# Another order for the first block: input weight, gate products and next attention

## The chip, the cores and the metric

The program runs on one core of a Trainium2 chip. The metric is the device time of one execution in microseconds (us); lower is better. TensorE multiplies (PE in the rows, PEld its weight loads), VectorE (DVE) and ScalarE (ACT) work on single elements and empty PSUM, GpSimd (POOL) helps with element work on SBUF, and SyncE (SP) issues the DMAs. Each engine takes its instructions strictly in the order in which they were recorded, and waits at the first whose inputs or buffers are not ready.

## The reference

Three layers follow each other on 8 batches of 576 rows and 512 features:

```
attn:  per head (8 x 64) and chunk of 64 rows:  softmax(q k^T / 8) v
moe:   h = relu(x @ w_in)              # 512 -> 1024, first half u, second half v
       v_n = (v - mean(v)) / sqrt(var(v) + 1e-6)
       v_s = w_spatial @ v_n + b_spatial[:, None]      # over the 576 rows
       x = (u * v_s) @ w_out                           # 512 -> 512
moe2:  u = x + (relu(x^T @ w_tok1) @ w_tok2)^T         # over the 576 rows
       out = u + relu(u @ w_ch1) @ w_ch2               # 512 -> 1536 -> 512
```

The moe weights arrive as 64-bit floats: as pairs of 32-bit words that the kernel turns into 32-bit floats itself.

## The kernel before

Every matrix is held as a sum of a rounded "hi" part and the remainder "lo", and each product is three matmuls (hi hi, hi lo, lo hi). Attention and the gated layer run block by block, one batch each: while TensorE does the gated layer of batch b, the other engines do the softmax of batch b+1 piece by piece. The order is written out by hand as three strings of words: `FIRST` (lines 24 to 36: attention of batch 0, gated layer of batch 0, conversion of the weights, attention of batch 1), `STEADY` (the same two layers for batches 1 to 6) and `LAST`. `play` (line 1168) reads a string and records the work of each word at once, so a string sets the order on every engine and on SP's DMA queue. The second mixer follows the strings.

The words that matter here; the number is a piece or a stage:

- Weight pieces of 512 KB, `wl` load (line 130), `wa` two passes on ScalarE that start the conversion (lines 144, 145), `wm` two passes on VectorE (153, 155), `we` an add on GpSimd (163), `wi` the hi part on ScalarE (185), `wk` the lo part on GpSimd or `wj` on VectorE (188). Pieces 0 to 3 are the second half of `w_in` (for v), 4 to 7 the first half (for u), 8 to 11 `w_out`.
- `gl`, `gt`, `gh`: the spatial weight loaded, transposed by TensorE (line 246) and split on ScalarE and VectorE (lines 83, 84). `gt` writes the same PSUM tile as the attention's last product `P` (tile `p`, one buffer), so either waits until the other has been emptied.
- Token products: `Y0` to `Y3` (v of four row groups, 12 matmuls each, line 536), `V2` (the rest, line 565). Emptying: `R` (line 583), `F`, `G` (the fold of the rest), `r` (statistics, lines 588 and 589), `rs`, `rq` (root of the variance), `N` (line 602), `i` and `Q` (hi and lo of the normed v, lines 608 and 617).
- `U0` to `U3`: products for u (24 matmuls, line 625), emptied by `E` (line 635). `W0` to `W3`: gate products (28 matmuls, line 648), then `M` (658), `H` (661), `J` (664). `A`, `B`, `O`: products with `w_out` (line 674), emptied by `D` (line 681), which also issues the store (line 682).
- Attention of the next batch: `L` loads a pair of heads (8 DMAs of 72 KB for q and k, line 297, and v, line 361), `x` transposes q and k on VectorE (line 377), `S` scores (391), `s` (410, 411), `e` exponential (417), `n` sums (421 to 423), `z` scaling on GpSimd (427), `T` transposes on TensorE (435), `t` empties them (443), `P` last product (459), `p` and `q` hi and lo (478, 480). `L4`, `L5`, `x4` in these words are already pairs 0 and 1 of the batch after the next. The same words with an `a` in front are batch 0's own attention.

PSUM: the tile `mm` for all the large products has two buffers, each of the attention's tiles has one. A raw weight piece sits in `craw` (two buffers), or, for pieces 0 to 3, in the space of the tiles g0 and g1, which the gate's result takes later.

Of the kernel before, what the change touches and what calls it, by code (L numbers as in the profile page):

```python
# [10 lines left out]
U32 = mybir.dt.uint32  # L11
# [12 lines left out]
FIRST = """  # L24
al0 wl0 al1 wl1 Z9 ax0 ay0 wa0 aS0 as0 ax1 al2 av0 wl2 wm0 ae0 ay1 an0 we0 az0 aS1 as1 wa1 aT0 wi0 wm1
at0 ax2 al3 av1 wl3 we1 wk0 ae1 ay2 an1 az1 aP0 aS2 ap0 as2 wi1 aq0 aT1 wa2 ae2 at1 ax3 av2 wm2 ay3 an2
az2 aP1 av3 aS3 as3 ap1 ae3 aq1 wj1 ax4 ay4 aT2 we2 wa3 wi2 at2 an3 wm3 az3 gl0 gl1 gl2 wl4 wl5 aP2 aS4
as4 ap2 wk2 we3 aq2 Y0 ae4 aT3 at3 wi3 an4 wk3 az4 Y1 aP3 L0 ap3 aq3 wa4 aT4 at4 Y2 aP4 wm4 ap4 aq4 Y3
x0 we4 wl6 wa5 L1 gt0 wi4 R0 R1 gh0 wm5 r0 S0 V2 s0 wk4 R3 we5 gt1 wi5 F r1 e0 R2 r3 wa6 G r2 gh1 wk5
U0 wl7 n0 x1 R4 z0 wm6 gt2 r4 we6 rs rq gh2 wi6 S1 U1 E0 wk6 s1 N0 T0 gt3 wa7 i0 Q0 t0 e1 gh3 N1 U2  # L30
wm7 n1 N2 we7 gt4 i1 wi7 E1 z1 Q1 gh4 wk7 i2 N3 N4 L2 wl8 U3 i4 Q2 x2 P0 p0 L3 S2 i3 E2 Q3 T1 q0 Q4
W0 t1 E3 s2 wl9 wa8 wm8 wa9 W1 we8 x3 e2 M0 M1 wi8
wm9 S3 W2 n2 wl10 we9 H0 wa10 W3 M2 s3 H2 wi9 J0 wl11 M3 z2 P1 S4 wk8 H1 J1 wj9 p1 q1 J2 H3
e3 wm10 T2 J3 A0 s4 n3 we10 A1 wa11 t2 L4 z3 wi10 B0 wm11 D0 e4 B1 P2 p2 D1 we11 T3 wj10 O2 n4
q2 t3 x4 z4 L5 P3 T4 wi11 p3 q3 D2 wk11 t4 O3 P4 D3 p4 q4
"""
STEADY = """
x1 ca L2 S0 V0 s0 e0 ca n0 z0 cm ce V1 cm S1 R1 r1 R0 r0 ce T0 R2 r2 R3 r3 t0 V2 U0 s1 e1
# [17 lines left out]
def attention_gmlp_mixer(  # L56
# [17 lines left out]
    DM = 512  # L74
# [1108 lines left out]
    pieces = by_rows(w_in, w_in_t, DM) + by_cols(w_in, w_in_t) + by_cols(w_out, w_out_t)  # L1183

    def load_piece(i):
        if i < 4:

            if i % 2 == 0:
                pieces[i].raw = pieces[i + 1].raw = lp.tile(
                    [128, 2, DM, 2], U32, tag=f"g{i // 2}", bufs=1, name="wv_raw")  # L1190
            pieces[i].load(pieces[i].raw[:, i % 2])
        else:
            pieces[i].load()

    class Stream:
# [19 lines left out]
    play(FIRST, {  # L1215
        **attn[0].ops("a"), **attn[1].ops(), **Gate(0).ops(), "Z": warm,
        "wl": load_piece, "wa": lambda i: pieces[i].start(), "wm": lambda i: pieces[i].mid(),
        "we": lambda i: pieces[i].end(), "wi": lambda i: pieces[i].to_hi(),
        "wj": lambda i: pieces[i].to_lo(nc.vector), "wk": lambda i: pieces[i].to_lo(nc.gpsimd),
# [34 lines left out]
    c1, s1 = {}, {}  # L1254
# [70 lines left out]
    for b in range(NB):  # L1325
        for n in range(21):
            g, i = divmod(n, 7)
# [9 lines left out]
    for n in range(7 * NB):  # L1337
        b, i = divmod(n, 7)
# [53 lines left out]
```

## Time and profile before

| what | us |
|---|---|
| median of 3 runs | 1244.7 (1242.97 to 1244.98) |
| the profiled execution | 1244.85 |
| its span, first to last instruction | 1242.3 |
| first attention score of `STEADY` begins | 118.42 |
| first gate product `W0` begins | 85.20 |

The profiled execution lies 0.15 us above the median. In the rows a time is counted from the span's start; "12 x12" style counts are instructions; "[3.18 <-ACT v L583]" behind an instruction is the engine's idle time just before it and what ended that. [...]

### The profile page before, as it was taken

How to read it: one execution, taken by the hardware profiler on the slowest of the kernel's cores; microseconds unless marked ns; L12 is line 12 of the kernel's file. 1: busy time of each engine (PE TensorE's matmuls, PEld its weight loads, DVE VectorE, ACT ScalarE, POOL GpSimd, SP SyncE). 2: the span in 40 equal slices, each digit the busy share in tenths (PEclk: the TensorE clock that was granted, in tenths of full speed). 3: DMA queues.
4: the chain of work that ended last, by engine and by line, in shares of the span. 5: the costliest groups of instructions: out<-in, count | busy, mean ns of one | idle time of the engine just before them, and what ended most of it. 6: DMA issues, size and time to landing. Idle time of an engine off the chain costs nothing. (4 is left out here: it accounts for less than half of the span.)

```text
span 1242.3 us, 25079 instructions
## 1 busy us (share of the span) xinstructions
PE 1192.9 (96%) x10042; PEld 1127.6 (91%) x10042; DVE 879.5 (71%) x1365; ACT 501.0 (40%) x797; POOL 161.7 (13%) x156
## 2 busy tenths in 40 slices
PE   6889999999999999998899999999998999999997
PEld 5779898989898989997889999999998999999997
DVE  5667757576766767366776776776768887787786
ACT  5464535354545444434332232332225434334431
POOL 2323111111121121013400000000005100000000
PEclk8889999999999999999989999999999999999999
DMA  9735537484838381178445565565385576666773
GB/s 228 150 77 127 96 104 134 100 172 107 200 85 206 89 213 38 56 158 203 140 142 170 170 189 172 163 187 166 134 303 190 195 217 199 183 188 189 214 213 45
DMA packets 405704, 196.00 MB, mean 158 GB/s; under 512 B 348434, under 2 KB 368338, under 8 KB 405588
## 3 DMA queue, kind: packets, MB, share of 16 engines
q1 hardware_dynamic: 400724, 193.81, 58.9%
q8 instruction: 79, 1.29, 0.5%
q10 hardware_dynamic: 4864, 0.59, 0.3%
q14 instruction: 37, 0.30, 0.1%
HBM read 123.16 MB, written 71.17 MB: 156 GB/s over the span
## 5 line engine op out<-in xcount | busy, mean ns | idle before, releaser
L1010 PE MATMUL ps_c<-ub,wt 128*128 128x288 f32 x2016 | 288.9, 298 | 6.6 <-ACT s L1042 2.5
L1010 PEld LDWEIGHTS ps_c<-ub,wt 128*128 128x128 f32 x2016 | 278.2, 190 | 12.9 <-ACT s L1042 3.8
L1010 PE MATMUL ps_c<-hb,wt 128*128 128x288 f32 x2016 | 268.9, 295 | 1.6 <-DVE hb L1099 1.6
L1010 PEld LDWEIGHTS ps_c<-hb,wt 128*128 128x128 f32 x2016 | 268.2, 188 | 2.2 <-DVE hb L1099 2.2
L625 PE MATMUL ps_u<-xt,w_in 128*128 128x288 f32 x768 | 110.3, 304 | 7.7 <-ACT ut L635 3.3
L625 PEld LDWEIGHTS ps_u<-xt,w_in 128*128 128x128 f32 x768 | 107.3, 195 | 9.1 <-ACT ut L635 3.5
L1098 ACT CAST hb<-h 128x1728 fp32r<-128x1728 f32 x40 | 64.8, 1638 | 122.7 <-DVE h L1091 50.0
L648 PE MATMUL ps_s<-ws,vn 128*128 128x288 f32 x768 | 108.5, 297 | 2.8 <-ACT ut L635 2.8
L648 PEld LDWEIGHTS ps_s<-ws,vn 128*128 128x128 f32 x768 | 103.5, 188 | 4.7 <-ACT ut L635 4.4
L674 PE MATMUL ps_o<-g,w_out 128*128 128x288 f32 x768 | 106.6, 296 | 0.0
L674 PEld LDWEIGHTS ps_o<-g,w_out 128*128 128x128 f32 x768 | 102.5, 188 | 1.0 <-ACT h L899 0.2
L1099 DVE TENSOR_TENSOR hb<-h,hb 128x1728 fp32r<-128x1728 f32 x40 | 78.2, 1955 | 28.6 <-ACT hb L1098 28.6
L536 PE MATMUL ps_v<-w_in,xt 128*128 128x512 f32 x384 | 92.7, 399 | 0.0
L536 PEld LDWEIGHTS ps_v<-w_in,xt 128*128 128x128 f32 x384 | 72.1, 190 | 16.7
L427 POOL TENSOR_TENSOR e<-e,sm 128x512 f32<-128x512 f32 (+1 forms) x40 | 39.1, 976 | 236.6 <-DVE sm L423 194.3
L163 POOL TENSOR_TENSOR ctmp<-ctmp,craw 128x512 uint32<-128x512 uint32 (+3 forms) x41 | 49.6, 1211 | 135.4 <-DVE ctmp L155 64.6
L926 PE MATMUL ps_u<-w,h 128*128 128x288 f32 x384 | 62.2, 299 | 4.4 <-DVE xh L931 4.4
L967 ACT CAST ub<-xh 128x576 fp32r<-128x576 f32 x56 | 37.4, 672 | 70.0 <-DVE xh L974 66.8
L926 PEld LDWEIGHTS ps_u<-w,h 128*128 128x128 f32 x384 | 54.8, 190 | 5.7 <-DVE xh L931 5.5
L968 DVE TENSOR_TENSOR ub<-xh,ub 128x576 fp32r<-128x576 f32 x56 | 43.0, 770 | 21.1 <-ACT ub L967 20.6
L868 ACT CAST xn<-nat 128x512 fp32r<-128x512 f32 x40 | 24.8, 619 | 76.8 <-DVE nat L866 75.6
L887 PE MATMUL ps_h<-xn,w 128*128 128x512 f32 x192 | 51.8, 403 | 3.4 <-ACT xn L868 3.3
(148 smaller groups left out, 1609.5 us busy)
## 6 DMA issues: line engine op xcount, KB each, us to landing
hd<-c SPq DMA_DIRECT2D x120, 288.0 KB, 2.2
h<-hd SPq DMA_DIRECT2D x40, 864.0 KB, 6.9
craw<-in_moe_w_ch_dram SPq DMA_DIRECT2D x24, 512.0 KB, 4.9
x_raw<-x2d SPq DMA_DIRECT2D x160, 64.0 KB, 2.7
xh<-x2d SPq DMA_DIRECT2D x16, 576.0 KB, 6.0
u2d<-xh SPq DMA_DIRECT2D x16, 576.0 KB, 3.1
u<-u2d SPq DMA_DIRECT2D x16, 576.0 KB, 6.8
x2d<-x2o SPq DMA_DIRECT2D x31, 288.0 KB, 2.9
```

The source lines that it names most:

```text
L163: nc.gpsimd.tensor_tensor(out=tu, in0=tu, in1=raw[:, :, 0], op=ALU.add)
L427: nc.gpsimd.tensor_tensor(out=e, in0=e, in1=sm.to_broadcast([128, e.shape[1], 64]), op=ALU.mult)
L536: nc.tensor.matmul(ps, lhsT=self.xt[kc][:, p, 128 * ti:128 * ti + 128], rhs=w_in_t[r][:, kc, DM:2 * DM], start=kc == 0 and n == 0, stop=kc ...
L625: nc.tensor.matmul(ps[:, h, 0:HALF], lhsT=w_in_t[r][:, kc, 128 * m:128 * m + 128], rhs=self.xt[kc][:, p, HALF * h:HALF * h + HALF], start= ...
L648: nc.tensor.matmul(ps[:, h, 0:HALF], lhsT=lhsT, rhs=rhs[:, HALF * h:HALF * h + HALF], start=n == 0, stop=n == len(ops) - 1)
L674: nc.tensor.matmul(ps[:, h, 0:HALF], lhsT=w_out_t[r][:, kc, 128 * m:128 * m + 128], rhs=self.g[p][:, kc, h], start=kc == 0 and n == 0, sto ...
L887: nc.tensor.matmul(ps[kk], lhsT=PB["w1"][r][:, m, ksl], rhs=xn[:, p], start=m == 0 and n == 0, stop=False)
L926: nc.tensor.matmul(ps, lhsT=h1[:, kk, p, 128 * m:128 * m + 128], rhs=PB["w2"][r][:, kk, HALF * h:HALF * h + HALF], start=n == 0, stop=n == 5)
L968: eng.tensor_tensor(out=lo, in0=x, in1=f32(hi), op=ALU.subtract)
L1010: nc.tensor.matmul(ps, lhsT=lhsT, rhs=rhs, start=first and n == 0, stop=n == len(ops) - 1, skip_group_check=True)
L1098: nc.scalar.copy(out=hi, in_=x)
L1099: nc.vector.tensor_tensor(out=lo, in0=x, in1=f32(hi), op=ALU.subtract)
```

## The change

Lines 3 to 10 of `FIRST` are written in another order, and the second pair of pieces of the first half of `w_in` (6 and 7) is loaded into the space of tile g0, where pieces 0 and 1 were; `craw` then is free for pieces 4 and 5 alone. All four loads `wl4` to `wl7` stand in a row; `wa4` to `wi6` stand between `Y0` and `R0`; `gt0` and `gt1` stand between the token products; `R0 R1 R3 R2` stand together; the four `W` are further apart in the string, with `S`, `T`, `P` of the next batch between them; `L4` stands behind `D1`.

```diff
-az2 aP1 av3 aS3 as3 ap1 ae3 aq1 wj1 ax4 ay4 aT2 we2 wa3 wi2 at2 an3 wm3 az3 gl0 gl1 gl2 wl4 wl5 aP2 aS4
-as4 ap2 wk2 we3 aq2 Y0 ae4 aT3 at3 wi3 an4 wk3 az4 Y1 aP3 L0 ap3 aq3 wa4 aT4 at4 Y2 aP4 wm4 ap4 aq4 Y3
-x0 we4 wl6 wa5 L1 gt0 wi4 R0 R1 gh0 wm5 r0 S0 V2 s0 wk4 R3 we5 gt1 wi5 F r1 e0 R2 r3 wa6 G r2 gh1 wk5
...
-e3 wm10 T2 J3 A0 s4 n3 we10 A1 wa11 t2 L4 z3 wi10 B0 wm11 D0 e4 B1 P2 p2 D1 we11 T3 wj10 O2 n4
-q2 t3 x4 z4 L5 P3 T4 wi11 p3 q3 D2 wk11 t4 O3 P4 D3 p4 q4
+az2 aP1 av3 aS3 as3 ap1 aq1 wj1 ae3 aT2 at2 ax4 ay4 we2 an3 wa3 wi2 az3 wm3 gl0 gl1 gl2 wl4 wl5 wl6 wl7
+aP2 aS4 as4 ap2 aq2 we3 Y0 ae4 wa4 an4 aT3 at3 wk2 az4 wi3 gt0 wm4 wk3 gh0 wa5 aP3 ap3 aq3 we4 wm5 Y1
+wi4 gt1 aT4 at4 gh1 wk4 we5 wa6 L0 Y2 wm6 aP4 ap4 aq4 wi5 wk5 we6 wa7 L1 Y3 x0 wi6 gt2 R0 R1 wm7 R3 R2
+r0 S0 gh2 r1 V2 F s0 r2 r3 G R4 e0 U0 r4 rs rq wk6 we7 gt3 n0 z0 gh3 N0 i0 N1 U1 E0 Q0 i1 wi7 x1 gt4 N2
+wk7 E1 Q1 i2 U2 T0 t0 gh4 N3 Q2 i3 S1 E2 N4 i4 Q3 L2 wl8 U3 s1 P0 e1 Q4 p0 E3 W0 q0 n1 z1 x2 L3 wl9
+wa8 S2 T1 t1 wm8 W1 s2 M0 P1 we8 e2 H0 p1 wi8 wa9 J0 q1 x3 wm9 n2 W2 S3 M1 z2 H1 s3 wk8 we9 J1
...
+q3 wl11 wa11 z4 wi10 A1 wm11 T4 t4 B0 we11 D0 wj10 P4 p4 B1 wi11 q4 D1 O2 wk11 L4 D2 x4 L5 O3 D3
...
     def load_piece(i):
-        if i < 4:
+        if i < 4 or 6 <= i < 8:
...
-                    [128, 2, DM, 2], U32, tag=f"g{i // 2}", bufs=1, name="wv_raw")
+                    [128, 2, DM, 2], U32, tag=f"g{i // 2 % 3}", bufs=1, name="wv_raw")
```

ScalarE around the emptying of the token products, before (`ps_v` are token products, `ps_w` a turned spatial weight, `w_in0` a hi part, `ctmp` a converted piece, `e` an exponential's tile):

```order
L583 ACTIVATE v32_162<-ps_v_535 128x512
L583 ACTIVATE v32_163<-ps_v_535 128x512
L83 CAST ws0_88<-ps_w_687 128x576
L583 ACTIVATE v32_165<-ps_v_536 128x512
L185 CAST w_in0_84<-ctmp_671 128x4x128
L574 COPY v_sum_744<-ps_v_720 64x512
L575 COPY v_sum_744<-ps_v_720 64x512
L417 ACTIVATE e_731<-e_731 128x512
L583 ACTIVATE v32_164<-ps_v_536 128x512
```

ScalarE at the same place, of the change (its lines are numbered one lower):

```order
L184 CAST w_in0_84<-ctmp_579 128x4x128
L143 ACTIVATE ctmp_686<-wv_raw_499 128x512
L144 ACTIVATE wv_raw_499<-wv_raw_499 128x512
L184 CAST w_in0_84<-ctmp_633 128x4x128
L582 ACTIVATE v32_162<-ps_v_537 128x512
L582 ACTIVATE v32_163<-ps_v_537 128x512
L582 ACTIVATE v32_165<-ps_v_538 128x512
L582 ACTIVATE v32_164<-ps_v_538 128x512
L82 CAST ws0_88<-ps_w_721 128x576
```

The four emptyings stand in a row, and the hi part of the third piece of the first half (`ctmp_633`, word `wi6`) now stands ahead of the first of them.

SP's queue at the end of `FIRST`, before (`qk_raw` are q and k of the batch after the next, `x2d0` the result of block 0):

```order
L297 DMA qk_raw_1348<-in_q_dram 32x18x32 x4
L297 DMA qk_raw_1353<-in_k_dram 32x18x32 x4
L361 DMA vt_1358<-in_v_dram 128x4x64 x2
L682 DMA x2d0_57<-x2o_1371 128x576
L682 DMA x2d0_57<-x2o_1400 128x576
L297 DMA qk_raw_1448<-in_q_dram 32x18x32 x4
```

SP's queue at the end of `FIRST`, of the change:

```order
L681 DMA x2d0_57<-x2o_1412 128x576
L681 DMA x2d0_57<-x2o_1440 128x576
L296 DMA qk_raw_1472<-in_q_dram 32x18x32 x4
L296 DMA qk_raw_1477<-in_k_dram 32x18x32 x4
L360 DMA vt_1482<-in_v_dram 128x4x64 x2
L681 DMA x2d0_57<-x2o_1485 128x576
```

The first two stores of block 0's result now stand ahead of the eight loads `L4` on the queue; before they stood behind them.

## Rows read from the trace of the kernel before

**Rows 1.** Windows: engines' busy us (instructions), PEclk, DMA share, GB/s.
```profile
70.00:80.00 10.00, 4.70 (x20) 4.02 (x21) 8.99 (x15) 5.67 (x10) 4.09 (x3) 0.64 0.01 2
86.00:118.00 32.00, 32.00 (x358) 30.90 (x357) 24.41 (x45) 15.63 (x29) 11.10 (x9) 1.00 0.52 115
118.00:1242.00 1124.00, 1096.51 (x9014) 1041.81 (x9012) 802.26 (x1216) 438.71 (x683) 123.03 (x119) 0.99 0.59 159
```

**Rows 2.** Timeline of PE: start, length, instruction, count, idle before and its releaser.
```profile
31.65 1.06 PE L459 MATMUL ps_p<-aT,vt 64*64 64x64 f32 x32 [3.56 <-ACT aT L443]
...
33.46 3.85 PE L536 MATMUL ps_v<-w_in,xt 128*128 128x512 f32 x12
...
37.50 3.02 PE L536 MATMUL ps_v<-w_in,xt 128*128 128x512 f32 x12
...
47.51 0.80 PE L246 MATMUL ps_w<-ident,ws_rows 128*128 128x128 f32 x5
...
55.25 4.98 PE L625 MATMUL ps_u<-xt,w_in 128*128 128x288 f32 x24 [3.18 <-ACT v L583]
...
61.87 3.46 PE L625 MATMUL ps_u<-xt,w_in 128*128 128x288 f32 x24
...
74.91 0.85 PE L625 MATMUL ps_u<-xt,w_in 128*128 128x288 f32 x2 [3.33 <-ACT ut L635]
76.95 5.65 PE L625 MATMUL ps_u<-xt,w_in 128*128 128x288 f32 x22 [1.20 <-POOL w_in L188]
...
83.24 1.10 PE L391 MATMUL ps_s<-qkT,qkT 64*64 64x64 f32 x32
...
85.20 3.46 PE L648 MATMUL ps_s<-ws,vn 128*128 128x288 f32 x24 [0.27 <-ACT ut L635]
...
118.42 1.10 PE L391 MATMUL ps_s<-qkT,qkT 64*64 64x64 f32 x32
```

**Rows 3.** Windows, where the granted clock was low: columns as in rows 1.
```profile
55.80:59.10 3.30, 3.30 (x15) 3.30 (x15) 2.47 (x7) 2.85 (x4) 0.27 (x1) 0.50 1.19 130
72.90:82.50 9.60, 6.40 (x24) 5.80 (x24) 7.41 (x13) 5.41 (x9) 3.57 (x3) 0.50 0.01 2
```

**Rows 4.** Timeline of ACT.
```profile
28.34 0.63 ACT L417 ACTIVATE e<-e 128x512 f32<-128x512 f32 x1 [2.28 <-DVE e L411]
...
31.00 0.59 ACT L443 COPY aT<-ps_t 128x512 f32<-128x512 f32 x1
...
57.38 1.28 ACT L598 ACT_TABLE_LOAD   x1
...
74.75 1.26 ACT L256 CAST ws_r<-ps_w 64x576 fp32r<-64x576 f32 x2
```

**Rows 5.** Groups by line, 0 to 119 us: busy us, mean ns of one, idle.
```profile
L163 POOL TENSOR_TENSOR ctmp<-ctmp,craw 128x512 uint32<-128x512 uint32 x8 | 11.1, 1382 | 38.2 <-issue 13.9 <-ACT aT L443 9.9 <-DVE ctmp L155 7.6
L188 POOL TENSOR_TENSOR w_in<-ctmp,w_in 128x512 fp32r<-128x512 f32 x7 | 9.8, 1406 | 8.7 <-ACT w_in L185 8.7
...
L377 DVE STREAM_TRANSPOSE qkT<-qk_raw 128x512 f32<-128x512 f32 x10 | 6.9, 686 | 0.0
...
L84 DVE TENSOR_TENSOR ws<-ps_w,ws 128x576 fp32r<-128x576 f32 x4 | 3.0, 758 | 5.1 <-ACT ws L83 5.1
```

**Rows 6.** Timeline of DVE and POOL: one VectorE pass beside GpSimd, one alone.
```profile
30.87 1.43 DVE L155 SCALAR_TENSOR_TENSOR ctmp<-wv_raw,ctmp 128x512 uint32<-128x512 uint32 x1
...
42.89 0.69 DVE L155 SCALAR_TENSOR_TENSOR ctmp<-craw,ctmp 128x512 uint32<-128x512 uint32 x1
...
30.71 1.04 POOL L427 TENSOR_TENSOR e<-e,sm 128x512 f32<-128x512 f32 x1 [2.09 <-ACT wv_raw L145]
```

**Rows 7.** Timeline of SP's queue, and the tile view of these eight loads.
```profile
63.10 2.63 SPq L297 DMA_DIRECT2D qk_raw<-in_q_dram  x4
65.77 2.12 SPq L297 DMA_DIRECT2D qk_raw<-in_k_dram  x4
...
DMA to landing us min/median/max: 3.0/3.5/4.0
```

More of the change, by code (lines that the diff above doesn't have):

```diff
@@ L26 @@
 at0 ax2 al3 av1 wl3 we1 wk0 ae1 ay2 an1 az1 aP0 aS2 ap0 as2 wi1 aq0 aT1 wa2 ae2 at1 ax3 av2 wm2 ay3 an2
-az2 aP1 av3 aS3 as3 ap1 ae3 aq1 wj1 ax4 ay4 aT2 we2 wa3 wi2 at2 an3 wm3 az3 gl0 gl1 gl2 wl4 wl5 aP2 aS4
-as4 ap2 wk2 we3 aq2 Y0 ae4 aT3 at3 wi3 an4 wk3 az4 Y1 aP3 L0 ap3 aq3 wa4 aT4 at4 Y2 aP4 wm4 ap4 aq4 Y3
-x0 we4 wl6 wa5 L1 gt0 wi4 R0 R1 gh0 wm5 r0 S0 V2 s0 wk4 R3 we5 gt1 wi5 F r1 e0 R2 r3 wa6 G r2 gh1 wk5
[L30 to L33, printed above, removed]
-e3 wm10 T2 J3 A0 s4 n3 we10 A1 wa11 t2 L4 z3 wi10 B0 wm11 D0 e4 B1 P2 p2 D1 we11 T3 wj10 O2 n4
-q2 t3 x4 z4 L5 P3 T4 wi11 p3 q3 D2 wk11 t4 O3 P4 D3 p4 q4
+az2 aP1 av3 aS3 as3 ap1 aq1 wj1 ae3 aT2 at2 ax4 ay4 we2 an3 wa3 wi2 az3 wm3 gl0 gl1 gl2 wl4 wl5 wl6 wl7
[4 more added lines that the diff above has]
+wa8 S2 T1 t1 wm8 W1 s2 M0 P1 we8 e2 H0 p1 wi8 wa9 J0 q1 x3 wm9 n2 W2 S3 M1 z2 H1 s3 wk8 we9 J1
+e3 T2 t2 W3 n3 M2 P2 z3 H2 p2 wi9 J2 q2 S4 T3 t3 M3 wl10 wa10 H3 s4 wj9 J3 e4 wm10 P3 we10 p3 A0 n4
+q3 wl11 wa11 z4 wi10 A1 wm11 T4 t4 B0 we11 D0 wj10 P4 p4 B1 wi11 q4 D1 O2 wk11 L4 D2 x4 L5 O3 D3
 """
```

## The prediction

> **What bounds the kernel now.** I read the windows first. From 86 us on TensorE is busy without a gap up to 118 us and for 1096.5 of the 1124 us after that [rows 1], so whatever the change wins or loses before the first score of the steady part (118.42 [rows 2]) goes through to the end one for one. The change touches nothing behind that. So only the first 118 us count, and in them the waits of TensorE, which the timeline of PE shows [rows 2]: 3.56 us before the third attention product, 3.18 before `U0`, 3.33 and 1.20 around `U3`, each ended by ScalarE or GpSimd. The windows with a low granted clock come next: after two of these waits TensorE runs at 0.50 of its clock [rows 3], so that `U0` takes 4.98 us where the next one takes 3.46 [rows 2]: 1.5 us on top. Between 70 and 80 us TensorE is busy 4.70 us of 10, VectorE 8.99 [rows 1]: there the chain runs over VectorE and ScalarE, and a reordering can move it but not make it shorter.
>
> **The change part by part.** I walked the changed rows of the engines by hand: each instruction starts when its engine has done the one ahead of it and the last of its inputs is there; durations are those of the rows (about 0.6 us on ScalarE [rows 4], 0.7 on VectorE, 1.4 on GpSimd [rows 5]). What comes out, on TensorE:
>
> 1. Third attention product. Its evacuation now follows the exponential (28.34 + 0.63 = 28.97, then 0.59) instead of standing at 31.00 behind the next weight piece [rows 4]: it can start at 29.5, 2.1 earlier. The first token product then meets no low clock: 3.02 instead of 3.85 [rows 2].
>
> 2. Token products. `gt0` (0.8) now stands between `Y0` and the fourth attention product, which writes the same PSUM tile and so waits for both halves of the split: ScalarE first has the start of piece 4, an evacuation and a hi part to do, then the cast of 0.6, then VectorE 0.76 [rows 5]. `gt0` ends at 34.8, the product starts at 37.05: a new wait of 2.2. `Y3` then ends at about 47.7, where it ended before (its successor starts at 47.51 [rows 2]), with two of five spatial transposes done more.
>
> 3. Emptying. `wi6` stands ahead of `R0` and needs GpSimd: hi of piece 5 at 45.4 (after the last attention piece is emptied), its lo part 1.28, the add of piece 6 1.3, the cast 0.6: `R0` at 49.2, the last of the four at 51.4. `U0` starts at 52.3 at the high clock, against 55.25 and 4.98 long [rows 2].
>
> 4. `U0` to `W0`. TensorE's work is 4 x 3.3 + 2 x 0.7 + 0.45 + 1.05 + 0.6 = 16.7 (four products, two spatial transposes, `T0`, `S1`, `P0`). VectorE sets four waits: `G` behind four statistics and the softmax (0.85), the split for `gt4` behind `rs` and `n0` and ScalarE's table load of 1.28 [rows 4] (0.95), `E0` behind `N0` and its cast (1.4), and `E2` behind the last spatial split, whose casts take 1.26 [rows 4] and two more of about 0.6 for the bias (0.7). So `W0` starts at 52.3 + 16.7 + 3.9 = 72.9, against 85.20 [rows 2]: 12.3 ahead. At that place the kernel before had done `S2` and `T1` already (1.10 from 83.24 on [rows 2], and some 0.35), 1.45 us: 10.8 ahead in work.
>
> 5. From `W0` on the kernel before has no wait [rows 1]; the change has five. `S2` stands directly behind `W0` and needs `x2`. On VectorE `x2` stands behind `q0`, which waits for ScalarE's `p0`, which stands behind the second table load and the exponential of `s1`, which VectorE starts only after the last spatial split. `x2` is 0.69 + 0.2 + 0.69 [rows 5], and its last result is there at 79.6, where `W0` ends at 76.8: 2.8. Then `T2` on `z2` 1.15, `P3` on `t3` 0.85, `T4` 0.35, `wj10` 0.5. Together 5.65: 5.15 ahead.
>
> 6. The end. `S0` of the steady part needs `x4`, and `x4` the loads `L4`, which now stand behind the stores of `D0` and `D1`. Let b be the end of `B1`. `D1` is emptied at b + 1.35 (ScalarE has a hi part to do), its store issued by b + 1.9; the eight loads take 65.77 + 2.12 - 0.5 - 63.10 = 4.3 from the first to the last issue and 3.5 to land [rows 7]; the transpose 0.8: b + 10.5. TensorE has `O2` and `O3`, 6.6 us, and 0.5 of the wait in step 5, so it is there at b + 7.1: a wait of 3.4. Bounds: 2.2 (landing in 3.0, ScalarE free) to 3.9 (landing in 4.0). I take 3.4: 1.75 ahead.
>
> 7. The clock. After waits of 3.18 and 3.33 it was low for what followed [rows 2, 3], so I expect it behind the 3.4 us before `S0`: 1.5, the price of `U0`. What is left is 0.25. For the shorter new waits (2.2, 2.8, and 0.95 and 1.4 with a short transpose between) the rows decide nothing: 0 to 1.5 each.
>
> The load of pieces 6 and 7 moves in front of `L0` and `L1` on SP; I cost that at nothing, since the queue issues such a group of eight in 4.8 us [rows 7] and the walk wants `x0` only at 46 us. If that cover is gone, each us of it is one of `S0` and `V2`.
>
> One piece of step 3 to 6 hangs on a neighbour. A pass of VectorE took 1.43 us while GpSimd ran beside it from 30.71 to 31.75, and 0.69 alone [rows 6]. [...] The change puts more of GpSimd's work beside VectorE's, so I have let such passes wait for GpSimd; without that the walk would come out about 0.85 earlier at b.
>
> **Rivals.**
>
> - The front gain is carried through (faster). `x2` and `L4` come in time, and only the 2.85 of small waits in step 5 is left: 10.8 - 2.85 = 8 ahead, 1236.9; one of the two alone gives 1239 to 1240. For it: the DMA engines are busy to 0.52 between 86 and 118 us [rows 1], and the walk may hold VectorE back too long. Against it: the queue order is fixed, and 4.3 us of issuing is longer than what is left of the 6.6.
> - The clock falls behind every new wait (slower). Four places (`P3`, `U2`, `S2`, `S0`), 1.5 us each: 1244.85 - 1.75 + 6.0 = 1249.1. It decides from the third fall on. For it: with waits of 3.33 and 1.20 and 0.85 of work between them [rows 2] it stayed at 0.50 for 9.6 us [rows 3]. Against it: the products between are 3 us long.
> - The change doesn't do what it says: piece 6 or 7 is not converted under the token products, since GpSimd takes 1.38 + 1.41 a piece [rows 5] and must also scale the attention, and `R0` comes some 2 us later: 1246.6.
>
> **How the numbers follow.** The sum is made against the profiled 1244.85, which is 0.15 above the median: 1244.85 - 0.25 = 1244.6, or 1244.4 against the median of 1244.7. Chances: this forecast 0.41 (its own range 1242 to 1247), gain carried through 0.27, clock 0.24, not done in time 0.08. Within 0.2%, 2.5 us, a measurement of this kernel can't tell a difference. The forecast's walk can be off by 2 us either way, which splits it 0.20 faster, 0.62 same, 0.18 slower; the first rival is faster; the second 0.15 same, 0.85 slower; the third 0.6 same, 0.4 slower. Faster 0.08 + 0.27 = 0.35; same 0.25 + 0.04 + 0.05 = 0.34; slower 0.07 + 0.20 + 0.03 = 0.31 (rounded so that they add up). The range reaches to one of two waits hidden, 1239, less half a us, and to the four falls, 1249.1, plus as much.
>
> **What would show it.** In the profile after: the third attention product near 29.5; 2 us of idle before the fourth, ended by the spatial split; `U0` near 52; `W0` near 73; an idle of 2 to 3 us before the third score, ended by VectorE's transpose; and one of about 3 us before the score that opens the steady part, ended by the transpose behind the last loads. If `W0` comes much later than 73, step 4 is wrong; if the last idle is under 1 us, step 6 is, and the kernel is faster. If TensorE has idle behind the opening score that it did not have before, the gain does not go through and the first paragraph is wrong.

## The result, and the profile after

The changed kernel is slower: median 1249.92 us of 4 executions (1247.15 to 1251.79), beside 1243.84 (1242.91 to 1244.98) of the kernel before. The ratio is 1.0050, 95% interval 1.0037 to 1.0063. I had forecast 1244.4, no change.

The profiled execution of the change is the fastest of its four, 1247.15 with a span of 1245.2; the three others, up to 4.6 us longer, left no trace. So the rows below explain 2.9 us of span (1245.2 against 1242.3), and the rest of the 6 us only as far as the experiments do.

First the timeline of TensorE (start, length, instruction, count, idle before it and what ended that), the rows that answer to [rows 2]:

```profile
27.79 0.70 PE L458 MATMUL ps_p<-aT,vt 64*64 64x64 f32 x32 [1.43 <-ACT aT L442]
...
28.95 3.06 PE L535 MATMUL ps_v<-w_in,xt 128*128 128x512 f32 x12
...
38.42 1.13 PE L458 MATMUL ps_p<-aT,vt 64*64 64x64 f32 x32 [4.97 <-DVE ws L83]
39.48 5.04 PE L535 MATMUL ps_v<-w_in,xt 128*128 128x512 f32 x12
...
66.52 3.46 PE L624 MATMUL ps_u<-xt,w_in 128*128 128x288 f32 x24 [0.92 <-ACT ut L634]
...
76.20 3.45 PE L647 MATMUL ps_s<-ws,vn 128*128 128x288 f32 x24 [0.70 <-ACT ut L634]
...
82.91 1.15 PE L390 MATMUL ps_s<-qkT,qkT 64*64 64x64 f32 x32 [2.73 <-DVE last L377]
...
119.52 1.97 PE L390 MATMUL ps_s<-qkT,qkT 64*64 64x64 f32 x32 [2.60 <-DVE qkT L376]
121.42 13.40 PE L535 MATMUL ps_v<-w_in,xt 128*128 128x512 f32 x48
134.75 1.15 PE L390 MATMUL ps_s<-qkT,qkT 64*64 64x64 f32 x32
```

The reader is to see two places. The fourth attention product at 38.42 waits 4.97, and the token product behind it takes 5.04 where the same work took 3.06 at 28.95. The opening score of the steady part at 119.52 waits 2.60 and takes 1.97 where the next one takes 1.15; the token products behind it then run slow too. The waits of the kernel before, 3.56, 3.18, 3.33 and 1.20 [rows 2], are gone or shorter: the third product comes at 27.79 and `W0` at 76.20 against 85.20. All of that lead and more is given back: the opening score starts 1.10 later than before (119.52 against 118.42).

The windows of the change (length, busy us with counts of PE, PEld, DVE, ACT, POOL, then the granted clock of TensorE as a share of its full one, DMA share, GB/s) show how fast TensorE ran there:

```profile
13.50:16.70 3.20, 2.79 (x35) 2.60 (x32) 2.26 (x5) 1.31 (x4) 1.38 (x2) 0.53 1.08 273
...
39.50:44.50 5.00, 5.00 (x18) 3.92 (x15) 2.81 (x3) 1.10 (x2) 2.72 (x3) 0.57 0.70 126
...
66.50:70.00 3.50, 3.48 (x26) 3.48 (x27) 3.25 (x7) 2.18 (x4) 1.30 (x1) 1.00 0.37 61
82.90:86.00 3.10, 3.09 (x48) 3.03 (x49) 2.79 (x5) 0.97 (x2) 1.31 (x1) 1.00 0.00 0
...
119.50:126.00 6.50, 6.48 (x43) 5.43 (x44) 1.51 (x4) 0.00 (x0) 0.00 (x0) 0.52 0.79 148
```

Over the windows behind the wait of 4.97 and behind that of 2.60 the granted clock is 0.57 and 0.52; behind the waits of 0.92 (66.50 on) and 2.73 (82.90 on) it is 1.00, though 2.73 is longer than 2.60. Before 26 us both programs do the same, but the clock was low for 3.2 us here (0.53) and for 7.0 us in the execution of before (0.52):

```profile
14.80:21.80 7.00, 5.72 (x81) 5.00 (x76) 4.42 (x8) 4.44 (x10) 4.61 (x4) 0.52 1.07 213
```

That gives this execution a lead of some 1.75 us which the change didn't earn (the exponential that [rows 4] has at 28.34 starts here at 26.63, 1.71 earlier).

Why the two places wait shows on ScalarE (and, in the last row, VectorE), on SP's queue, and in the tile view of the loads of 112 to 118 us:

```profile
34.83 0.66 ACT L143 ACTIVATE ctmp<-craw 128x512 f32<-128x512 f32 x1 [2.76 <-DMA craw<-in_moe_w_in_dram]
35.39 0.66 ACT L144 ACTIVATE craw<-craw 128x512 uint32<-128x512 uint32 x1
35.95 0.57 ACT L442 COPY aT<-ps_t 128x512 f32<-128x512 f32 x1
36.41 0.62 ACT L184 CAST w_in<-ctmp 128x512 fp32r<-128x512 f32 x1
36.93 0.64 ACT L82 CAST ws<-ps_w 128x576 fp32r<-128x576 f32 x1
...
37.61 0.76 DVE L83 TENSOR_TENSOR ws<-ps_w,ws 128x576 fp32r<-128x576 f32 x1 [0.93 <-ACT ws L82]
```

```profile
28.55 0.94 SPq L129 DMA_DIRECT2D craw<-in_moe_w_in_dram  x2
...
109.89 2.36 SPq L681 DMA_DIRECT2D x2d<-x2o  x2
112.29 2.12 SPq L296 DMA_DIRECT2D qk_raw<-in_q_dram  x4
114.45 2.13 SPq L296 DMA_DIRECT2D qk_raw<-in_k_dram  x4
```

```profile
DMA to landing us min/median/max: 2.5/2.6/2.7
```

`wa4` (L143) waits 2.76 us for the load of piece 4, which SP issued at 28.55, behind three loads of spatial weight (2 x 576 + 144 KB, 1.3 MB); it is used 6.3 us later. ScalarE took its work in the string's order: the transposes of the spatial weight were done at 33.45, but the two passes, an evacuation and a hi part went ahead of the cast of the spatial split (L82, 36.93), and all of them stood behind that load. VectorE's half of the split (L83, 37.61) needs the cast, and the product needs VectorE's half. At the other place the eight loads `L4` are issued from 112.29 to 116.58, behind the two stores, and land 2.6 us later; VectorE's transpose of 0.7 follows, and TensorE starts at 119.52.

### The profile page after: what moved, and what is told of

Its sections match the earlier page's. It is cut to its first block, busy times and chain, and to the rows that moved or that the text cites. A ratio compares the mean times of both kernels' runs of the same rounds, so it can differ in the third digit from the quotient of the medians.

```text
span 1245.2 us, 25092 instructions
## 1 busy us (share of the span) xinstructions
PE 1189.1 (95%) x10042; PEld 1122.8 (90%) x10042; DVE 881.6 (71%) x1365; ACT 501.2 (40%) x797; POOL 160.7 (13%) x156
## 5 line engine op out<-in xcount | busy, mean ns | idle before, releaser
L624 PE MATMUL ps_u<-xt,w_in 128*128 128x288 f32 x768 | 105.7, 296 | 1.6 <-ACT ut L634 0.9
L624 PEld LDWEIGHTS ps_u<-xt,w_in 128*128 128x128 f32 x768 | 103.3, 189 | 2.6 <-ACT ut L634 1.1
L535 PE MATMUL ps_v<-w_in,xt 128*128 128x512 f32 x384 | 96.0, 409 | 0.0
L162 POOL TENSOR_TENSOR ctmp<-ctmp,craw 128x512 uint32<-128x512 uint32 (+3 forms) x39 | 47.1, 1209 | 106.2 <-DVE ctmp L154 57.7
```

The source lines that it names most:

```text
L162: nc.gpsimd.tensor_tensor(out=tu, in0=tu, in1=raw[:, :, 0], op=ALU.add)
L535: nc.tensor.matmul(ps, lhsT=self.xt[kc][:, p, 128 * ti:128 * ti + 128], rhs=w_in_t[r][:, kc, DM:2 * DM], start=kc == 0 and n == 0, stop=kc ...
L624: nc.tensor.matmul(ps[:, h, 0:HALF], lhsT=w_in_t[r][:, kc, 128 * m:128 * m + 128], rhs=self.xt[kc][:, p, HALF * h:HALF * h + HALF], start= ...
```

## The experiments

Times are medians; each ratio is to the kernel before, run beside it on the same chip. Differences to the change (1249.92) are taken between medians of different times; the kernel before stood at 1243.84 beside the change, at 1243.80 beside the first four kernels below, and at 1243.2 and 1243.1 beside the others, so up to 0.7 us of such a difference can be the time at which it was measured. Each trace is of one execution: the fastest of its kernel for the change, the late loads in the kernel before and the last kernel, a middle one for the first kernel with fillers, and the slowest or second slowest for the rest. In the kernels below, when a word moves in the string, the work moves on every engine.

**The loads in front of the stores.** Only `L4` moves, to its place ahead of `A1`.

```diff
-q3 wl11 wa11 z4 wi10 A1 wm11 T4 t4 B0 we11 D0 wj10 P4 p4 B1 wi11 q4 D1 O2 wk11 L4 D2 x4 L5 O3 D3
+q3 wl11 L4 wa11 z4 wi10 A1 wm11 T4 t4 B0 we11 D0 wj10 P4 p4 B1 wi11 q4 D1 O2 wk11 D2 x4 L5 O3 D3
```

> The change with one word moved: the loads L4 stand ahead of D0's store instead of behind D1. Theory (two queue waits of block 0, each followed by a low clock, make the loss): the wait of 2.60 before the opening score of the steady part goes, and with it the 2.0 + 0.9 us that the low clock costs in the products behind it: 2.6 to 5.5 us under the changed kernel's median of 1249.9, that is 1244.4 to 1247.3. Rival (the loss is made behind the first block, where the shifted work meets other transfers): within 1 us of 1249.9.

Measured: 1243.85 (1239.92 to 1246.27), ratio 1.0004 [0.9992, 1.0015]: 6.1 us less than the change, a little over what was expected. TensorE's timeline of this kernel:

```profile
38.91 1.13 PE L458 MATMUL ps_p<-aT,vt 64*64 64x64 f32 x32 [5.38 <-DVE ws L83]
...
66.57 4.98 PE L624 MATMUL ps_u<-xt,w_in 128*128 128x288 f32 x24 [0.92 <-ACT ut L634]
...
84.48 1.97 PE L390 MATMUL ps_s<-qkT,qkT 64*64 64x64 f32 x32 [2.72 <-DVE last L377]
...
119.87 1.15 PE L390 MATMUL ps_s<-qkT,qkT 64*64 64x64 f32 x32
```

The wait at the opening score is gone, and the score takes 1.15. The rows above it are as telling: the waits of 0.92 and 2.72 are those of the change to the hundredth, but here what follows runs slow (4.98 against 3.46, 1.97 against 1.15):

```profile
67.00:70.60 3.60, 3.60 (x18) 3.60 (x18) 2.78 (x6) 1.72 (x4) 1.27 (x1) 0.54 0.47 76
84.40:87.60 3.20, 3.12 (x38) 3.03 (x39) 2.07 (x5) 0.07 (x1) 1.28 (x1) 0.50 0.00 0
```

So behind the same waits the clock was 0.54 and 0.50 in this execution and 1.00 in that of the change. One profile doesn't price a wait; the median of several executions does.

**The spatial split in front of piece 4.** `wa4` moves from behind `ae4` to behind `gh0`, its VectorE passes to behind the attention piece.

```diff
-aP2 aS4 as4 ap2 aq2 we3 Y0 ae4 wa4 an4 aT3 at3 wk2 az4 wi3 gt0 wm4 wk3 gh0 wa5 aP3 ap3 aq3 we4 wm5 Y1
+aP2 aS4 as4 ap2 aq2 we3 Y0 ae4 an4 aT3 at3 wk2 az4 wi3 gt0 wk3 gh0 wa4 aP3 ap3 aq3 wm4 wa5 we4 wm5 Y1
```

> The change with wa4 and wm4 behind gh0: ScalarE splits the first spatial transpose before it waits for the load of piece 4. Theory: the wait of 4.97 before the fourth attention product becomes some 1.5, and the clock stays up there (2.4 us in the product and in Y1): 3.4 to 5.8 us under 1249.9, that is 1244.1 to 1246.5. Rival (loss behind the first block): within 1 us of 1249.9. If conversion under the token products is the bound after all, the time comes back before R0 and the gain is under 1 us.

Measured: 1244.05 (1242.27 to 1246.4), ratio 1.0005 [0.9996, 1.0013]: 5.9 us less than the change. Its TensorE:

```profile
35.53 0.69 PE L458 MATMUL ps_p<-aT,vt 64*64 64x64 f32 x32 [1.52 <-DVE ws L83]
36.16 4.61 PE L535 MATMUL ps_v<-w_in,xt 128*128 128x512 f32 x12
...
62.75 4.97 PE L624 MATMUL ps_u<-xt,w_in 128*128 128x288 f32 x24 [0.90 <-ACT ut L634]
...
80.65 1.97 PE L390 MATMUL ps_s<-qkT,qkT 64*64 64x64 f32 x32 [2.72 <-DVE last L377]
...
118.66 1.97 PE L390 MATMUL ps_s<-qkT,qkT 64*64 64x64 f32 x32 [2.52 <-DVE qkT L376]
```

The wait falls from 4.97 to 1.52. Even behind that the token product was slow in this execution (4.61, at a granted clock of 0.50 from 37 to 39 us), where I had expected the clock to stay up, and the wait at the opening score is there as in the change. All four waits that the clock rival of the prediction names are thus still in this kernel, and in this execution what follows runs slow behind each of them: behind the 0.90 before `U2` (4.97, where the change took 3.46) and the 2.72 before `S2` (1.97, where it took 1.15) too, each of these at a price of 1.5 us (up to the transposes behind `U2`, and up to the end of the gate product behind `S2`). The profiled execution of the kernel with the load of piece 4 in front, further down, shows the same at all four.

**Both.**

> The change with both moves (L4 ahead of D0's store, split ahead of piece 4). Theory: the gains add, 6 to 11 us under 1249.9: 1239 to 1244, at or under the kernel before (1243.8). Rival (loss behind the first block): 1249. If the two are one wait that only moves, no better than the better of the two alone.

Measured: 1239.85 (1238.67 to 1240.53), ratio 0.9966 [0.9954, 0.9978]: 10.1 us less than the change and faster than the kernel before. Its TensorE:

```profile
36.56 0.69 PE L458 MATMUL ps_p<-aT,vt 64*64 64x64 f32 x32 [1.87 <-DVE ws L83]
37.19 3.05 PE L535 MATMUL ps_v<-w_in,xt 128*128 128x512 f32 x12
...
114.06 1.15 PE L390 MATMUL ps_s<-qkT,qkT 64*64 64x64 f32 x32
115.14 11.41 PE L535 MATMUL ps_v<-w_in,xt 128*128 128x512 f32 x48
```

Here neither place has a low clock behind it (behind the 2.72 before `S2` the clock did fall, to 0.50 from 80 to 82 us), and the opening score starts at 114.06, 5.5 before the change. That settles where the loss was made: at these two queues, and not behind the first block, which is the same in all three kernels.

**The late loads in the kernel before.** `L4`, `x4` and `L5` of the kernel before stand behind `D1`, nothing else is changed.

```diff
-e3 wm10 T2 J3 A0 s4 n3 we10 A1 wa11 t2 L4 z3 wi10 B0 wm11 D0 e4 B1 P2 p2 D1 we11 T3 wj10 O2 n4
-q2 t3 x4 z4 L5 P3 T4 wi11 p3 q3 D2 wk11 t4 O3 P4 D3 p4 q4
+e3 wm10 T2 J3 A0 s4 n3 we10 A1 wa11 t2 z3 wi10 B0 wm11 D0 e4 B1 P2 p2 D1 we11 T3 wj10 O2 n4
+q2 t3 z4 P3 T4 wi11 p3 q3 L4 D2 x4 L5 wk11 t4 O3 P4 D3 p4 q4
```

> The kernel before with one part of the change alone: L4 and x4 stand behind D1 as in the change. Theory: the opening score of the steady part waits about 2 us for x4, and the clock may fall behind it (up to 2.9): 2 to 5 us over the kernel before, 1246 to 1249. Rival (loss behind the first block, not from this wait): the same as before, 1243.8 within 1 us.

Measured: 1244.84 (1241.92 to 1246.94), ratio 1.0006 [0.9996, 1.0017]: a miss. Its opening score:

```profile
116.75 1.15 PE L391 MATMUL ps_s<-qkT,qkT 64*64 64x64 f32 x32 [1.28 <-DVE qkT L377]
```

The wait is only 1.28, and the clock stayed up behind it in this execution, the fastest of its twelve (the score took 1.15, `V0` behind it 11.43). TensorE has more work behind `B1` in this string, 9.2 us (106.29 to 115.47, `P2` to `P4`) where the change has 6.6 (`O2` and `O3`). What late loads cost is thus a matter of what else stands there; in the kernel before this run shows none that can be measured.

**The waits kept, the clock held up.** To the change are added matmuls whose result nobody reads (`K`, with their count), in front of the waits: 16 before the fourth attention product, 3 before `U2`, 9 before `S2`, 10 before the opening score. The waits stay as they were; TensorE works in them.

```diff
+    def keep(n):
+        ps = ps_at.tile([128, 512], F32, tag="s", bufs=1, name="ps_k")
+        for _ in range(n):
+            nc.tensor.matmul(ps, lhsT=w_in_t[0][:, 0, DM:DM + 128],
+                             rhs=w_in_t[0][:, 0, DM:2 * DM], start=True, stop=True)
...
-... gh0 wa5 aP3 ...  Q1 i2 U2 T0 ...  wa8 S2 T1 ...  L5 O3 D3
+... gh0 wa5 K16 aP3 ...  Q1 i2 K3 U2 T0 ...  wa8 K9 S2 T1 ...  L5 O3 D3 K10
```

> The change with all its waits kept, and matmuls whose result nobody reads put into four of them on TensorE: 16 before the fourth attention product, 3 before U2, 9 before the third score, 10 before the opening score. Theory (the clock is a part of the loss of its own): no low clock behind these places, and 2.4 + 1.5 + 0.9 + 2.9 us of slower products go as far as they fell: 3 to 7 us under 1249.9, that is 1243 to 1247, with the waits as long as before (fillers and idle together). Rival (the low clock is hidden behind the waits of other engines): within 1 us of 1249.9.

Measured: 1243.52 (1240.54 to 1246.63), ratio 0.9998 [0.9987, 1.0009]: 6.4 us less than the change. Its TensorE, and one window:

```profile
33.72 3.91 PE L1186 MATMUL ps_k<-w_in 128*128 128x512 f32 x16
38.40 0.69 PE L458 MATMUL ps_p<-aT,vt 64*64 64x64 f32 x32 [0.77 <-DVE ws L83]
39.02 3.05 PE L535 MATMUL ps_v<-w_in,xt 128*128 128x512 f32 x12
...
116.97 1.15 PE L390 MATMUL ps_s<-qkT,qkT 64*64 64x64 f32 x32 [0.22 <-DVE last L377]
118.05 11.42 PE L535 MATMUL ps_v<-w_in,xt 128*128 128x512 f32 x48
```

```profile
26.00:119.00 93.00, 84.72 (x876) 74.00 (x876) 64.93 (x127) 50.00 (x95) 29.90 (x25) 1.00 0.53 120
```

The fourth product starts at 38.40 as in the change (38.42): the wait is as long, from 33.72 on. But the token product behind it takes 3.05 in place of 5.04, `V0` behind the opening score 11.42, and the granted clock is 1.00 from 26 to 119 us, where the change has 0.96. Taking away the falls of the clock, with the waits in place, gives back as much as the change had lost.

**The load of piece 4 in front of the spatial weight.**

```diff
-az2 aP1 av3 aS3 as3 ap1 aq1 wj1 ae3 aT2 at2 ax4 ay4 we2 an3 wa3 wi2 az3 wm3 gl0 gl1 gl2 wl4 wl5 wl6 wl7
+az2 aP1 av3 aS3 as3 ap1 aq1 wj1 ae3 aT2 at2 ax4 ay4 we2 an3 wa3 wi2 az3 wm3 wl4 gl0 gl1 gl2 wl5 wl6 wl7
```

> The change with the load of piece 4 issued ahead of the spatial weight's three, ScalarE's order as it is. Theory (ScalarE waits for this load, and the split stands behind it): the wait before the fourth attention product falls from 4.97 to some 2 to 3.5, since the spatial weight now lands about 1.5 later: 1.5 to 5 us under 1249.9. Rival (the split waits for the emptying and the hi part on ScalarE, not for the load): unchanged, 1249.9 within 1 us.

Measured: 1246.07 (1241.11 to 1249.77), ratio 1.0024 [1.0011, 1.0036]: 3.85 us less than the change. Its ScalarE, then its TensorE:

```profile
33.04 0.67 ACT L143 ACTIVATE ctmp<-craw 128x512 f32<-128x512 f32 x1
```

```profile
36.79 0.69 PE L458 MATMUL ps_p<-aT,vt 64*64 64x64 f32 x32 [2.58 <-DVE ws L83]
37.41 4.62 PE L535 MATMUL ps_v<-w_in,xt 128*128 128x512 f32 x12
```

`wa4` doesn't wait for its load, and the product's wait is 2.58, near the 2.2 that the prediction had for a load that is there. The other 2.4 of the change's 4.97 are that load. In this execution the work behind all four waits was slow: 4.62 behind this one, 4.98 behind 0.91 (`U2`), 1.87 behind 2.71 (`S2`) and 1.98 behind 2.56 (opening score).

**The same fillers in the kernel before.** `K10` before its third attention product, `K8` before `U0`, `K11` before `U3`.

```diff
-... wl4 wl5 aP2 ...  U0 wl7 n0 ...  wl8 U3 i4 ...
+... wl4 wl5 K10 aP2 ...  K8 U0 wl7 n0 ...  wl8 K11 U3 i4 ...
```

> The kernel before with its waits kept and matmuls whose result nobody reads in three of them: 10 before the third attention product, 8 before U0, 11 before U3. It asks how much of the time before was low clock, so that before and change can be compared at the high clock (the change with fillers: 1243.5). Theory: 0.8 + 1.5 + 2.2 us of slower products go as far as they fell, 1239 to 1242; the change's waits are then longer than those of before by 2 to 4 us. Rival (the kernel before loses nothing to the clock, its waits hide it): 1243.2 to 1244, and the change at the high clock is no worse than before.

Measured: 1241.24 (1239.2 to 1244.84), ratio 0.9985 [0.9975, 0.9995]: 1.9 us less than the kernel before. One fall is left, behind a wait inside `U3` that no filler covers: 22 matmuls take 4.71 where the 24 of `U2` take 3.45, at a granted clock of 0.50 from 76 to 79 us.

```profile
75.32 4.71 PE L625 MATMUL ps_u<-xt,w_in 128*128 128x288 f32 x22 [1.51 <-POOL w_in L188]
```

By these medians the clock costs the kernel before some 1.9 and the change some 6.4, so about 4.5 of the 6.1 us between them is the clock. Both prices are rough: with the fillers too the mean clock over the whole span differs from execution to execution (0.988 to 0.995 here, 0.990 to 0.996 for the change). With fillers in both, the intervals of the two (0.9998 [0.9987, 1.0009] and 0.9985 [0.9975, 0.9995]) overlap; whether the rest, 1.6, is waits that are longer in sum is not settled.

**More words moved.** To both moves above is added: `L2` and `x2` earlier, so that `S2` doesn't wait behind `W0`.

```diff
-... Q1 i2 U2 T0 t0 gh4 ...  Q3 L2 wl8 U3 ...  n1 z1 x2 L3
+... Q1 i2 L2 U2 T0 t0 x2 gh4 ...  Q3 wl8 U3 ...  n1 z1 L3
```

> c_both with x2 ahead of the last spatial split, in an idle stretch of VectorE. Theory (the third score waits for x2 alone): its wait of 2.72 goes, T1 then waits about 1 for z1, so 1.5 to 2.7 us under c_both's 1239.85, and less low clock: 1237 to 1238.5. Rival (the wait only moves to T1 in full): 1239.5 to 1240.

Measured: 1236.83 (1234.86 to 1238.48), ratio 0.9944 [0.9931, 0.9958], 0.2 below what was expected. `S2` has no wait left (`T1` behind it waits 1.36):

```profile
76.10 1.15 PE L390 MATMUL ps_s<-qkT,qkT 64*64 64x64 f32 x32
```

Then, on top of it, `wi6` behind the emptying and `E0` ahead of `N0`:

```diff
-... Y3 x0 wi6 gt2 R0 R1 wm7 R3 R2 ...  gh3 N0 i0 N1 U1 E0 Q0 i1
+... Y3 x0 gt2 R0 R1 wm7 R3 R2 wi6 ...  gh3 E0 N0 i0 N1 U1 Q0 i1
```

> g_x2 with wi6 behind R2 and E0 ahead of i0. Theory: V2's wait of 0.75 goes, the statistics start about 1.5 us earlier and U2's wait of 0.9 shrinks, so W0 comes 1 to 2.5 us earlier than in g_x2: 1235 to 1237.5. Rival (VectorE's chain from the statistics to the last split is the bound, not where ScalarE starts it): within 0.5 us of g_x2.

Measured: 1234.04 (1232.74 to 1235.98), ratio 0.9926 [0.9913, 0.9939], 1 us below what was expected and faster than both kernels. Its TensorE:

```profile
67.83 3.46 PE L647 MATMUL ps_s<-ws,vn 128*128 128x288 f32 x24 [0.71 <-ACT ut L634]
...
107.11 1.15 PE L390 MATMUL ps_s<-qkT,qkT 64*64 64x64 f32 x32
```

`W0` stands at 67.83 and the opening score at 107.11, 11.3 us before that of the kernel before, 1.8 of which this execution had from its start by the clock (at 0.50 from 13 to 16 us alone; the exponential of [rows 4] at 26.50 against 28.34).

## Why the prediction was wrong

The first paragraph held in the main. The score at 134.75 is 3.96 later than its counterpart of before (130.79), and the one at 186.80 still 3.96 (182.84). At the end of the span the difference is 2.9. "One for one" is thus too strong: nearly all of the 1.06 is regained in the second mixer, by 670 us (667.67 against 670.75, 3.08), where TensorE has waits of up to 2.1 before and 2.9 in the change, and the clock falls behind some of them. There too like waits had both behind them: behind 2.10 (at 605.38) the kernel before took 1.81 and 2.50 for its next two groups of matmuls (granted clock 0.62 from 605.4 to 609.7), behind 2.12 (at 608.79) the change took 1.06 and 1.76 for the same (1.00 from 608.8 to 613). From the second steady score to the end of the span the traces of all the kernels here take between 1110.4 and 1114.8 us, the change 1110.45 and the kernel before 1111.5.

To hold the steps against the trace, the predicted times are first taken 1.75 earlier, for the start that this execution had by the clock before 26 us (the 1.75 that step 6 left as the gain is another one, and happens to be as large).

| step | predicted | less 1.75 | measured |
|---|---|---|---|
| 1, third product | 29.5 | 27.75 | 27.79 |
| 2, wait before the fourth | 2.2 | | 4.97 |
| 2, fourth product | 37.05 | 35.3 | 38.42 |
| 4, `W0` | 72.9 | 71.15 | 76.20 |
| 5, wait for `x2` | 2.8 | | 2.73 |
| 6, wait at the opening score | 3.4 | | 2.60 |
| 6, opening score (118.42 - 1.75) | 116.67 | 114.92 | 119.52 |
| 7, low clock behind it | 1.5 | | 2.86 |

- Steps 1 and 5 (its largest wait) were right to a tenth, and nearly so the sums of step 4 (`U0` to `W0` 20.6, measured 20.06) and of what lies between `W0` and the opening score (43.77, measured 43.32). Step 3 was right too: from the end of `Y3` to `U0` it had 4.6, measured 4.45, so the third rival (pieces not converted in time) did not come. Walking the words engine by engine does work. The prediction's sign "If `W0` comes much later than 73, step 4 is wrong" pointed at the wrong step: `W0` came 5.05 late, all of it from before `U0`.
- **Step 2 failed**, by 2.8. The walk let ScalarE start piece 4 as soon as its queue was free, and asked for no time at which the load would be there. In the kernel before the same load stood behind the same spatial weight, but its user stood later, so no row showed a wait. The sentence "I cost that at nothing" looked at pieces 6 and 7 only. The experiments with the load in front (2.58) and with the split in front (1.52) show the load as the cause of the excess, and ScalarE's order as the cause of 0.7 to 1.1 more; what is left (1.52, and 1.87 with both moves) stays with the split itself.
- **Step 7 failed**, in number and in size: one fall of the clock at 1.5 was counted. The profiled execution has two: behind the fourth product, 0.4 in it and 2.0 in the token product, and behind the opening score, 0.87 in it and 1.99 in `V0` (13.40 against the 11.41 of the kernel with both moves). With these the account of this execution closes: 1244.6 - 1.75 = 1242.85 was predicted for it; 4.6 later at the opening score and 1.36 more of low clock give 1248.8; the 1.06 regained, and 0.6 less outside the span (1.95 against 2.55), give its 1247.15.
- The rival "the clock falls behind every new wait" (1249.1) had the right mechanism and, against the median, nearly the right time; the closeness is in part luck, since it has the 2.2 of step 2 for a wait of 4.97, and 1.5 for falls that cost 2.4 and 2.86. The clock fell behind two of its four waits in the profiled execution of the change, but behind all four in those of the kernels with the split in front and with the load in front, at 1.5 each behind `U2` and `S2`, as the rival had it. The kernel with the waits kept and the clock held up shows that this mechanism is there, at 6.4 us, some 4.5 more than in the kernel before. For short waits the prediction said that the rows "decide nothing", and then counted them at none.
- Step 6 was right in kind and 0.8 too long: the loads landed 2.6 us after issue (2.5 to 2.7), where 3.5 had been taken from a busier stretch [rows 7] (DMA share 0.81 while these were issued, from 112.3 to 116.6, against 1.01 from 63.1 to 67.9 before).
- The rival "gain carried through" (1236.9) is what the kernel with these waits removed gives: 1236.83. That the two agree to a tenth is chance (its executions lie between 1234.86 and 1238.48, and it has the split in front besides).
- The 0.85 that the walk takes for VectorE's passes beside GpSimd was my estimate from one pass of [rows 6], and no run shows it. In the change one such pass (L154) took 1.41 from 29.34 on, with GpSimd busy from 29.00 to 30.21; the eleven others up to 119 us, which began with GpSimd idle, took 0.69.

What remains open: the three other executions of the change are 1.7 to 4.6 us longer than the profiled one, at mean clocks of 0.985 to 0.987 against 0.989. No trace of them was taken, so what follows is an estimate from the others: falls behind `U2` and `S2`, as in the two kernels that keep these waits, would add 3.0 us, and a start without this execution's lead 1.75, together 4.75. That is enough for all three, but is not shown for any.

The runs show no length of a wait from which on the clock falls. Behind the 4.97 at 38.42 the token product took 5.04, where the same work took 3.06 at 28.95. Behind 0.90 `U2` took 4.97 in one execution (the split in front) and 3.44 in another (both moves), and behind 2.72 and 2.73 the score `S2` took 1.97 (the loads in front) and 1.15 (the change).

## What to carry to other kernels

In the change, a step that waited for a load held up all that is recorded behind it on its engine (2.76 us of ScalarE): before moving such a step forward, count the bytes ahead of its load on the queue, and record what the bounding engine waits for ahead of it. Loads for the next stage do not belong behind stores that wait for the end of this one, where little other work is left (a wait of 2.60 in the change with 6.6 us of work, 1.28 in the kernel before with 9.2). A new wait of TensorE costs its length and, in some executions, the slower products behind it (1.4 to 2.9 us a fall here), so price it by both and measure it over several executions.

## What the runs showed of the hardware

- With matmuls whose result nobody reads put into the waits, the granted clock was 1.00 from 26 to 119 us (0.96 in the change), and the median was 6.4 us lower with the waits in place.
- The same work, with the same waits to the hundredth (0.92 and 2.72 or 2.73), had the clock at 1.00 behind them in one execution and at 0.50 to 0.54 in that of a kernel that differs only further on.
- A fall of the clock behind a wait cost 1.5 us at `U2` and at `S2` wherever it came, 1.6 to 2.4 at the fourth attention product and 1.4 to 2.9 at the opening score (1.4 in the kernel with the load in front, whose fall was shorter there).
- A load of 512 KB, issued right behind 1.3 MB of others, was there 6.3 us after its issue; 72 KB loads landed in 2.6 where the DMA share was 0.81 while they were issued, and in 3.5 where it was 1.01.
